# Weights loaded ahead of batch 1, and chunk 0's feed-forward ahead of and among batch 1's attention

## The chip, the cores and the metric

One core of one Trainium2 chip runs the kernel. The metric is the device time of one execution in microseconds (us); the median of three runs stands for a kernel. TensorE is called PE below, its weight load PEld, VectorE DVE, ScalarE ACT, GpSimd POOL and SyncE SP.

## The reference

Eight batches of eight heads, 576 tokens, head size 64. Attention looks back over a window of 128 tokens and has a bias that falls with distance; its output, 4608 tokens by 512, goes through a feed-forward layer with 2048 inner columns.

```python
scores = scale * np.matmul(q, k.transpose(0, 1, 3, 2))
mask = (rel >= 0) & (rel < window)
scores = np.where(mask, scores + bias[None], -1000000000.0)
attn = exp(scores - max) / sum
x = (attn @ v), heads side by side            # 4608 x 512
h = x @ w_in                                  # 512 -> 2048
g = h * np.clip(h + 3.0, 0.0, 6.0) / 6.0
out = g @ w_out                               # 2048 -> 512
```

## The kernel before, in words

**Attention** goes by head pairs g = 0 to 31, four to a batch. A window of 128 means that each block of 128 queries sees two blocks of keys, its own ("diag") and the one before ("off"). For each pair: q and k are brought to bf16 and transposed to have the head's 64 columns on the partitions (`qTb`, `kTb`); `scores` (L344) multiplies them on PE into PSUM tiles of pool `ps_sc`; ACT takes exponentials into `pd`, `po` and a small `p4buf` (L384, L409); POOL zeroes what the mask forbids (L405, L414); `values` (L444) or, in batches 0 and 1, `attend` (L456) multiplies with v on PE and divides on DVE; `back` (L471) transposes the result into `xT`, the feed-forward's input, on PE for the first batches and by a DMA transpose from SP later.

**The feed-forward** goes by chunks of 512 tokens, nine in all (`nt`). `moe_up` (L512) is one block of 128 inner columns: four matmuls into one PSUM bank, an ACT operation (L520) that reads the bank, and a DVE operation (L521) that reads both and writes `gbuf`. There are 16 ups to a chunk. Their banks are two tiles of pool `ps_h` (tag "h"), which `transposes`, `double` and late `back`s use too; chunk 0 alone also takes one of `ps_av` and `ps_o` for some (`UP_BANKS`, L510). `moe_down` (L538) is a quarter of the 16 matmuls of 128 tokens' output: 16 steps to a chunk, with `gbuf` as weights; after each fourth, DVE copies the bank to `osb` and SP stores it.

**The order of the work** is written out by hand. Every engine executes its instructions in the order in which the code issues them. `units` (L566) lists ups and downs in one line, by order strings (`ORDER`, L563: U an up of chunk nt, D a down of chunk nt − 1), and `fill(n)` (L573) issues the next n of them; an up is held back until the attention of its tokens is done. `first_batch` (L608), `second_batch` (L667) and `segment` (L717, pairs 8 to 32) place the fills among the attention's pieces. In `segment` a pair has seven places for them, `f[0]` to `f[6]`: after the scores, after each of the two diagonal exponentials, after each of the two others, and two at the end; the pieces of `values` of the pair before stand ahead of `f[2]` and `f[4]`. `FILLS` (L715) gives seven units to pairs 9 to 11 and 13 to 15, the default eight to the others.

**The loads.** Batch 0's q and k come as runs of nine tokens a partition (`load_run`, L90), v by tokens (`load_tokens`, L108). Batch 1's q and k come as float32 runs of two pairs (`load_double`, L96) on SP's queue, are cast by POOL (`prepare_double`, L224) and transposed nine blocks of 128 at a time (`wide_double`, L249). The weights come as four column groups of w_in (`load_w_in`, L165) and four row groups of w_out (`load_w_out`, L170), cast to bf16 on their way by DMAs that POOL issues: w_in 0 during batch 0's attention, w_in 1 to 3 among batch 1's preparations, w_out ahead of the last pair of batch 1. Batch 0 keeps its `pd` and `po` in the room of `w_out_sb`, batch 1 in `gbuf[1]` (`rooms`, L275).

Of the kernel before, what the change touches and what calls it, by code (L numbers as in the profile page):

```python
# [10 lines left out]
FP32 = mybir.dt.float32  # L11
# [7 lines left out]
def kernel(  # L19
# [145 lines left out]
    def load_w_in(g):  # L165
        nc.gpsimd.dma_start(
            out=w_in_sb[:, :, ts(g, 512)],
            in_=moe_w_in[:, ts(g, 512)].rearrange("(k p) f -> p k f", p=128))

    def load_w_out(g):  # L170
        nc.gpsimd.dma_start(
            out=w_out_sb[:, ts(g, 4), :],
            in_=moe_w_out[ds(g * 512, 512), :].rearrange("(m p) d -> p m d", p=128))

    def second_w_in():
        nc.gpsimd.memset(w_out_sb[:, 4, 0:1], 0.0)
        load_w_in(1)
        load_w_in(2)
# [45 lines left out]
    def prepare_double(b, dp, copies, nms="kq", early=None):  # L224
        for nm, copy in zip(nms, copies):
            pr = prs.tile([128, RT, 2 * D], BF16, tag=f"pr{nm}", name="pr2")
            for e in range(2):
                copy(out=pr[:, :, ts(e, D)],  # L228
                     in_=ldbuf["qk".index(nm)][:, ds((2 * dp + e) * RT * D, RT * D)].rearrange(
                         "p (t d) -> p t d", t=RT))  # L230
# [307 lines left out]
    def moe_down(nt, step):  # L538
        sub, part = divmod(step, 4)
        if nt == n_nt - 1 and sub == 3:  # L540
            if part == 3:
                last_rows(nt, sub)
            return
        if part == 0:
            if nt == n_nt - 1 and sub in (1, 2) or nt == 1 and sub == 0:
                ops[nt, sub] = ps_h.tile([128, d_model], FP32, tag="h", name="ops")
            else:
                ops[nt, sub] = ps_o.tile([128, d_model], FP32, tag="o", name="ops")
        for i in range(4):
            ms = part * 4 + i  # L550
            nc.tensor.matmul(ops[nt, sub], lhsT=gts[nt][:, ms, ts(sub, 128)],  # L551
                             rhs=w_out_sb[:, ms, :], start=(ms == 0), stop=(ms == n_ms - 1))
# [13 lines left out]
    units = [(0, moe_up, step) for step in range(16)]  # L566
    for nt in range(1, n_nt + 1):
        ups, downs = iter(range(16)), iter(range(16))
        for c in "".join(ORDER[0 if nt == 1 else 2 if nt == n_nt else 1]):
            units.append((nt, moe_up, next(ups)) if c == "U" else (nt, moe_down, next(downs)))  # L570
    at = [0]

    def fill(n):  # L573
        for _ in range(n):
            if at[0] == len(units):
                return
            nt, fn, step = units[at[0]]
            if fn is moe_up and done[0] < NP * (min((nt * NT + NT - 1) // S, B - 1) + 1):
                return
            fn(nt if fn is moe_up else nt - 1, step)  # L580
            at[0] += 1

    V, P, A = nc.vector.tensor_copy, nc.gpsimd.tensor_copy, nc.scalar.copy
# [24 lines left out]
    def first_batch():  # L608
        prepare(0, (V, A))
        warm_up(20)  # L610
        tables_diag(0)
        warm_up(9)
        transposes(0, (V, A))
        tables_off(0)
        scores_diag(0)
        prepare(1, (P, V))
        transposes(1, (V, V))
        scores_off(0)
        exp_full(0)
# [21 lines left out]
        for dp in range(2):  # L641
            for nm in "kq":
                load_double(1, dp, nm, nc.sync)
        load_tokens(1, "v")
# [17 lines left out]
        done[0] = NP  # L662
        fill(1)
        wide_double(1, 0, "k", A)
        fill(2)

    def second_batch():  # L667
        for g in range(NP, 2 * NP - 1):
            if g < NP + 2:
                wide_double(1, 1, "kq"[g - NP], V)  # L670
            scores_diag(g)
            exp_diag(g, 0)
            exp_diag(g, 1)
            fill(1 if g == NP + 2 else 2)
            scores_off(g)
            exp_off_full(g)
            fill(2 if g == NP + 2 else 1)
            if g == NP + 1:
                cast_tokens(1, "v")
        for i in range(4):  # L680
            load_w_out(i)
        g = 2 * NP - 1
        scores(g)
        exp_diag(g, 0)
        exp_diag(g, 1)
# [7 lines left out]
        exp_off_full(g)  # L693
        fill(1)
        attend(NP)
        fill(1)
        attend(NP + 1)
        fill(1)
        back(NP)
        attend(NP + 2)  # L700
        fill(1)
# [62 lines left out]
    with tc.manual_schedule(engines=every):  # L764
        load_run(0, "k", nc.scalar)
        load_run(0, "q", nc.sync)
        load_run(1, "k", nc.scalar)
        load_run(1, "q", nc.sync)
        for g in (2, 3):
            load_run(g, "k", nc.scalar)  # L770
            load_run(g, "q", nc.sync)
        load_tokens(0, "v")
        constants()
        memsets()
        memsets_later()
        first_batch()
        second_batch()
        fill(2)
# [33 lines left out]
```

## Time and profile before

| what | value |
|---|---|
| median of three runs | 321.34 us (320.37 to 321.56) |
| the profiled execution's own time | 320.53 us |
| its span in the trace | 318.8 us |
| PE busy | 309.7 us, 97% |
| ACT busy | 195.8 us, 61% |
| DVE busy | 173.2 us, 54% |
| POOL busy | 140.8 us, 44% |
| mean granted clock of PE | 1.0 |

The page of a profile names groups of instructions by the line of the code, the engine, the operation, and what is written from what (`hps<-xT,w_in_sb`). Rows in order of time have the start, the length of the merged group in us, the line and, in square brackets, how long the engine stood idle before it and what released it. Rows of waits have the waiting engine, line and tile, what it waited for, then the total, the number of waits and the longest in us. Matmuls are pipelined: a group's length includes the end of its last matmul, so the distance from one start to the next is the measure of what a group costs.

### The profile page before, as it was taken

To read this page: it belongs to the slowest core of one execution; us is meant where nothing else is said; L and a number is where in the kernel's file an instruction comes from. 1 tells how busy PE (TensorE), PEld (TensorE's weight loads), DVE (VectorE), ACT (ScalarE), POOL (GpSimd) and SP (SyncE) were. 2 spreads that over 40 slices of the span, in tenths; PEclk is the share of its full clock that TensorE was granted. 3 is DMA by queue.
4 is the path that set the end of the run, shared out by engine and by line. 5 is a ranking of instruction groups with operands and counts; after the bars stand their busy time and mean duration, and the time that the engine had idled before them with its cause. 6 is when DMAs were issued, how large, how long until landed. Compare 5 with 4: busy or idle time off the path is not lost.

```text
span 318.8 us, 7860 instructions
## 1 busy us (share of the span) xinstructions
PE 309.7 (97%) x3143; PEld 165.3 (52%) x3143; DVE 173.2 (54%) x338; ACT 195.8 (61%) x334; POOL 140.8 (44%) x249
## 2 busy tenths in 40 slices
PE   7879999999999999999999999999999999999996
PEld 6565465455555444444677644444444444444443
DVE  6667675554456654655565556555656455455510
ACT  3758977877767775766676667666764244244401
POOL 7465493684494776276736663663331000000000
PEclk9999999999999999999999999999999999999999
DMA  7999999999999989999999999933112100000112
GB/s 269 208 334 217 246 272 188 246 240 175 197 263 183 206 198 220 187 192 239 218 208 205 234 197 196 244 78 72 41 36 88 53 34 35 33 33 35 66 56 76
DMA packets 131428, 51.95 MB, mean 163 GB/s; under 512 B 118976, under 2 KB 123328, under 8 KB 131392
## 3 DMA queue, kind: packets, MB, share of 16 engines
q1 hardware_dynamic: 126160, 45.36, 70.2%
q0 software_dynamic: 4224, 4.19, 8.3%
q10 hardware_dynamic: 1008, 1.90, 1.7%
q8 instruction: 24, 0.39, 0.6%
q14 instruction: 12, 0.10, 0.1%
HBM read 36.70 MB, written 9.44 MB: 145 GB/s over the span
## 4 chain that ended last, share of the span: by engine, by line
PE 86%; ACT 5%; DMA 3%; DVE 2%; issue 1%; SPq 1%; POOL 0%; POOLq 0%; ACTq 0%
PE ops L551 37%; PE hps L501 36%; PE sce L364 2%; DMA ldbuf<-in_q_dram 2%; PE av L441 2%; ACT r L520 2%; PE av L433 2%; PE ops L532 1%; DVE gbuf L521 1%; PE w L153 1%; DMA xT<-avs 1%; PE tp L220 1%; PE tp L255 1%; ACT kTb L245 1%; SPq L98 1%
## 5 line engine op out<-in xcount | busy, mean ns | idle before, releaser
L521 DVE SCALAR_TENSOR_TENSOR gbuf<-r,hps 128x512 bf16<-128x512 f32 x144 | 98.8, 687 | 100.8 <-ACT r L520 99.6
L520 ACT ACTIVATE r<-hps,bias 128x512 f32<-128x512 f32 x144 | 99.0, 689 | 86.4 <-PE hps L501 86.1
L501 PE MATMUL hps<-xT,w_in_sb 128*128 128x512 bf16 (+1 forms) x640 | 145.1, 358 | 1.1 <-ACT xT L488 0.3
L551 PE MATMUL ops<-w_out_sb,gbuf 128*128 128x512 bf16 x560 | 137.8, 379 | 0.0
L501 PEld LDWEIGHTS <-w_in_sb 128*128 128x128 bf16 x640 | 59.3, 98 | 55.4 <-issue 1.3
L551 PEld LDWEIGHTS <-gbuf 128*128 128x128 bf16 x560 | 51.8, 98 | 55.5
L414 POOL TENSOR_SCALAR_AFFINE_SELECT po<-po 128x512 bf16<-128x512 bf16 x48 | 30.3, 636 | 32.9 <-ACT po L412 32.7
L405 POOL TENSOR_SCALAR_AFFINE_SELECT pd<-pd 128x512 bf16<-128x512 bf16 x48 | 29.8, 634 | 29.6 <-ACT pd L388 29.5
L388 ACT ACTIVATE pd<-sce,bias_d 128x512 bf16<-128x512 f32 x48 | 31.7, 685 | 5.3 <-POOL tbuf L195 4.0
L195 POOL CAST tbuf<-ldbuf 128x512 bf16<-128x512 f32 (+1 forms) x45 | 25.6, 614 | 19.7 <-issue 10.4
L560 DVE COPY osb<-ops 128x512 f32<-128x512 f32 x33 | 22.7, 688 | 19.7 <-PE ops L551 19.6
L412 ACT ACTIVATE po<-sce,bias_o 128x512 bf16<-128x512 f32 x48 | 33.0, 688 | 0.0
L452 DVE TENSOR_TENSOR avs<-av,rc 128x384 bf16<-128x384 f32 (+1 forms) x48 | 23.6, 491 | 1.6
L441 PEld LDWEIGHTS <-pd 128*128 128x128 bf16 x192 | 14.4, 97 | 8.3 <-issue 0.5
L433 PE MATMUL av<-vbuf,po 128*128 128x65 bf16 x192 | 18.1, 193 | 0.0
L441 PE MATMUL av<-vbuf,pd 128*128 128x65 bf16 x192 | 17.5, 194 | 0.3 <-ACT kTb L245 0.3
L433 PEld LDWEIGHTS <-po 128*128 128x128 bf16 x192 | 14.3, 98 | 3.0 <-DVE avs L452 0.5
L188 POOL CAST vbuf<-ldbuf 128x1024 bf16<-128x1024 f32 x14 | 14.2, 1043 | 3.5 <-DMA ldbuf<-in_v_dram 3.5
L417 ACT ACTIVATE p4buf<-sce,bias_d 128x64 bf16<-128x64 f32 x48 | 15.5, 323 | 0.0
L228 POOL CAST pr<-ldbuf 128x576 bf16<-128x576 f32 x20 | 12.9, 670 | 5.0 <-DMA ldbuf<-in_q_dram 2.1
L451 DVE RECIPROCAL rc<-av 128x6 f32<-128x6 f32 (+1 forms) x48 | 8.8, 183 | 4.3 <-PE av L441 4.3
L364 PEld LDWEIGHTS <-kTb 64*32 64x32 bf16 x736 | 6.2, 91 | 8.7 <-issue 7.6
(104 smaller groups left out, 211.7 us busy)
## 6 DMA issues: line engine op xcount, KB each, us to landing
out_dram<-osb SPq DMA_DIRECT2D x33, 256.0 KB, 2.5
ldbuf<-in_v_dram SPq DMA_DIRECT2D x32, 256.0 KB, 5.2
ldbuf<-in_q_dram SPq DMA_DIRECT2D x20, 256.0 KB, 4.7
ldbuf<-in_k_dram SPq DMA_DIRECT2D x16, 256.0 KB, 4.8
ldbuf<-in_q_dram SPq DMA_DIRECT2D x12, 288.0 KB, 7.2
ldbuf<-in_k_dram SPq DMA_DIRECT2D x12, 288.0 KB, 6.5
w_in_sb<-in_moe_w_in_dram POOLq DMA_DIRECT2D x4, 512.0 KB, 9.3
w_out_sb<-in_moe_w_out_dram POOLq DMA_DIRECT2D x4, 512.0 KB, 10.4
```

The costliest lines, as they stand in the source:

```text
L195: nc.gpsimd.tensor_copy(out=tbuf[:m, :, j, :], in_=s[:m, j, :, :].rearrange("p (i e) d -> p i (e d)", e=2))
L388: nc.scalar.activation(out=pd[:, e, :, :], in_=st["sce"][e][:, :, 0, :], func=ACT.Exp, bias=bias_d[:, h:h + 1], scale=scale)
L405: nc.gpsimd.affine_select(out=pd[:, e, :, :], in_=pd[:, e, :, :], pattern=[[0, 4], [1, 128]], channel_multiplier=-1, base=0, compare_op=AL ...
L412: nc.scalar.activation(out=po[:, e, :, :], in_=sc[:, :, 1, :], func=ACT.Exp, bias=bias_o[:, h:h + 1], scale=scale)
L414: nc.gpsimd.affine_select(out=po[:, e, :, :], in_=po[:, e, :, :], pattern=[[0, 4], [-1, 128]], channel_multiplier=1, base=-1, compare_op=A ...
L433: nc.tensor.matmul(out_av, lhsT=po[:, e, qt % 4 if full(g) else qt - 1, :], rhs=vb[:, qt - 1, h, :], start=True, stop=False)
L441: nc.tensor.matmul(out_av, lhsT=d, rhs=vb[:, qt, h, :], start=(qt == 0), stop=True)
L452: nc.vector.tensor_tensor(out=st[g, "avs"][:, qts[0]:qts[0] + nq, :, :], in0=av[:, 0:nq, :, 0:D], in1=rc[:, 0:nq, :, :].to_broadcast([128, ...
L501: nc.tensor.matmul(hps[:, lo:hi], lhsT=w_in_sb[:, ks, ts(ms, 128)], rhs=xT[:, ks, ds(src, hi - lo)], start=(ks == 0), stop=(ks == n_ks - 1))
L520: nc.scalar.activation(out=r6, in_=hps, func=ACT.Relu, bias=bias3[:, 0:1], scale=1.0 / 6.0)
L521: nc.vector.scalar_tensor_tensor(out=gts[nt][:, ms, :], in0=r6, scalar=1.0, in1=hps, op0=ALU.min, op1=ALU.mult)
L551: nc.tensor.matmul(ops[nt, sub], lhsT=gts[nt][:, ms, ts(sub, 128)], rhs=w_out_sb[:, ms, :], start=(ms == 0), stop=(ms == n_ms - 1))
```

## The change

All four groups of w_in are now issued by POOL during batch 0's attention, and all four of w_out right behind batch 0's last `back`. Batch 1's q and k follow on the same queue, pair by pair, as runs that the DMA casts to bf16 (`cast_run`), and are transposed in blocks of 64 by `transposes`, which batch 0 already uses. Batch 1's v and batch 2's q and k are loaded by SP after a one-element POOL copy that reads pair 5's k.

Chunk 0's 16 ups are issued in one `fill(16)` ahead of batch 1, its downs in `FIRST`'s order ahead of and among batch 1's attention; the fills between batch 1's attends go. Banks of some downs change (`BESIDE`, and `ps_av` for odd 128s of chunk 0). In the new order strings U is an up of the chunk, d a down of the same chunk, D one of the chunk before. Pairs 8 to 12 get six units, 13 to 24 seven, 25 on eight.

```diff
+    crun = ctx.enter_context(tc.tile_pool(name="crun", bufs=4))
...
+    def cast_run(g, nm):
+        b, hp = divmod(g, NP)
+        pr = crun.tile([128, RT * D], BF16, tag=f"cr{nm}", name="cr")
+        nc.gpsimd.dma_start(out=pr, in_=src_of[nm][b, 2 * hp:2 * hp + 2, :, :].rearrange(
+            "e (p t) d -> (e p) (t d)", t=RT))
+        st[g, nm] = pr
...
-    ORDER = [("UUDUDUUDUD", "UUDUDUDUD", "UDUDUDD", "UUDDDD"),
-             ("DDDD", "UUDUDUDUD", "UUDUDUDUD", "UUDUDUDDUU"),
-             ("DDDD",) * 4]
...
+    BESIDE = {(1, 1), (1, 3), (2, 1), (3, 0), (4, 0), (n_nt - 1, 1), (n_nt - 1, 2)}
+    FIRST = [0, 4, 1, 5, 2, 6, 3, 7, *range(8, 16)]
...
+    units = [(0, moe_up, step) for step in range(16)] + [(0, moe_down, step) for step in FIRST]
+    late = "DDDD", "UUDUDUDUDUUDUDUDUDUUDUDUDDUU"
+    early = {1: "UUUUd" * 4 + "d" * 12, 2: "UUUUd" * 4 + "d" * 8, 3: "UUUUD" * 4 + "d" * 8,
+             4: "UUD" * 8 + "dddd", 5: late[1], n_nt: "D" * 16}
...
+        for i in range(1, 4):
+            load_w_in(i)
...
-        prepare_double(1, 0, (P, P), early=second_w_in)
...
-        wide_double(1, 0, "q", V)
-        prepare_double(1, 1, (P, P))
-        load_w_in(3)
+        for i in range(4):
+            load_w_out(i)
+        for g in range(NP, 2 * NP):
+            for nm in "kq":
+                cast_run(g, nm)
+        nc.gpsimd.tensor_copy(out=ldbuf[3][0:1, 0:1], in_=st[NP + 1, "k"][0:1, 0:1])
+        load_tokens(1, "v")
...
+        fill(16)
...
+        fill(8)
+        transposes(NP, (V, A))
...
+            if g < 2 * NP - 1:
+                transposes(g + 1, (V, V))
...
-    FILLS = {g: (1, 1, 1, 2, 0, 1, 1) for g in (9, 10, 11, 13, 14, 15)}
+    FILLS = {g: (1, 1, 1, 1, 0, 1, 1) for g in range(8, 13)}
+    FILLS |= {g: (1, 1, 1, 2, 0, 1, 1) for g in range(13, 25)}
```

More of the change, by code (lines that the diff above doesn't have):

```diff
@@ L173, in load_w_out @@
             in_=moe_w_out[ds(g * 512, 512), :].rearrange("(m p) d -> p m d", p=128))
[L175 to L178, printed above, removed]
     def cast_v(b, j, copy):
@@ L544, in moe_down @@
         if part == 0:
-            if nt == n_nt - 1 and sub in (1, 2) or nt == 1 and sub == 0:
+            if (nt, sub) in BESIDE:
                 ops[nt, sub] = ps_h.tile([128, d_model], FP32, tag="h", name="ops")
+            elif nt == 0 and sub % 2 == 1:
+                ops[nt, sub] = ps_av.tile([128, d_model], FP32, tag="av", name="ops")
             else:
@@ L561, in moe_down @@
                 nc.sync.dma_start(out=out[rows, :], in_=osb)
-    ORDER = [("UUDUDUUDUD", "UUDUDUDUD", "UDUDUDD", "UUDDDD"),
-             ("DDDD", "UUDUDUDUD", "UUDUDUDUD", "UUDUDUDDUU"),
-             ("DDDD",) * 4]
-    units = [(0, moe_up, step) for step in range(16)]
+    BESIDE = {(1, 1), (1, 3), (2, 1), (3, 0), (4, 0), (n_nt - 1, 1), (n_nt - 1, 2)}
+    FIRST = [0, 4, 1, 5, 2, 6, 3, 7, *range(8, 16)]
+    steps = [iter(range(16)) for _ in range(n_nt)], [iter(range(16)) for _ in range(n_nt)]
+    units = [(0, moe_up, step) for step in range(16)] + [(0, moe_down, step) for step in FIRST]
+    late = "DDDD", "UUDUDUDUDUUDUDUDUDUUDUDUDDUU"
+    early = {1: "UUUUd" * 4 + "d" * 12, 2: "UUUUd" * 4 + "d" * 8, 3: "UUUUD" * 4 + "d" * 8,
+             4: "UUD" * 8 + "dddd", 5: late[1], n_nt: "D" * 16}
     for nt in range(1, n_nt + 1):
-        ups, downs = iter(range(16)), iter(range(16))
-        for c in "".join(ORDER[0 if nt == 1 else 2 if nt == n_nt else 1]):
-            units.append((nt, moe_up, next(ups)) if c == "U" else (nt, moe_down, next(downs)))
+        for c in early.get(nt, late[0] + late[1]):
+            at = nt - (c == "D")
+            units.append((at, moe_up, next(steps[0][at])) if c == "U" else
+                         (at, moe_down, next(steps[1][at])))
     at = [0]
@@ L579, in fill @@
                 return
-            fn(nt if fn is moe_up else nt - 1, step)
+            fn(nt, step)
             at[0] += 1
@@ L640, in first_batch @@
         cast_v(0, 4, P)
[L641 to L644, printed above, removed]
+        for i in range(1, 4):
+            load_w_in(i)
         attend(0)
@@ L662, in first_batch, with second_batch @@
         done[0] = NP
+        fill(16)
+    def second_batch():
+        fill(8)
+        transposes(NP, (V, A))
         fill(1)
[L664 to L670, printed above, removed]
+        for g in range(NP, 2 * NP):
             scores_diag(g)
@@ L673, in second_batch @@
             exp_diag(g, 1)
-            fill(1 if g == NP + 2 else 2)
+            if g < 2 * NP - 1:
+                transposes(g + 1, (V, V))
+            fill(1)
             scores_off(g)
             exp_off_full(g)
[L677 to L685, printed above, removed]
+            fill(2 if g == NP else 1 if g < 2 * NP - 1 else 0)
+            for j, copy in {NP: (), NP + 1: ((0, V), (1, P)), NP + 2: ((2, V),),
+                            NP + 3: ((3, V), (4, P))}[g]:
+                cast_v(1, j, copy)
         prepare_double(2, 0, (P, P))
@@ L777 @@
         second_batch()
-        fill(2)
         segment(2 * NP, G, lambda g: FILLS.get(g, (1, 1, 1, 2, 0, 1, 2)))
```

5 lines of the change are left out of this document (removed).

## Prediction

> **What bounds the kernel now.** I read the page first (busy shares, slices), then PE's own waits, then PE, ACT and DVE side by side in the order of time, last the queue of SP.
>
> ```profile
> span 318.8 us, 7860 instructions
> PE 309.7 (97%) x3143; PEld 165.3 (52%) x3143; DVE 173.2 (54%) x338; ACT 195.8 (61%) x334; POOL 140.8 (44%) x249
> PE   7879999999999999999999999999999999999996
> ...
> PE scd L297 <- DVE kTb L221: 0.9, 3, 0.4
> ...
> PE av L441 <- ACT kTb L245: 0.3, 2, 0.2
> ...
> PE hps L501 <- DVE gbuf L521: 0.3, 1, 0.3
> ...
> PE hps L501 <- DMA xT<-avs: 0.3, 1, 0.3
> ...
> PE tp L255 <- POOL pr L228: 0.2, 1, 0.2
> PE tb L482 <- DVE avs L452: 0.2, 1, 0.2
> PE tp L243 <- ACT kTb L245: 0.2, 1, 0.2
> ```
>
> The reader is to see that PE is the bound: 97% busy, and of its waits the largest group has 0.9 us in three, the longest 0.4 (the rows left out are smaller, but for 1.4 us at the very start). The work of PE stays nearly the same under the change, so the change can win very little, and every wait that it makes on PE is lost for good: nothing after it makes up for it. So the question is only which waits go and which come.
>
> The unit of the feed-forward part is one up (four matmuls of L501) or one down (four of L551).
>
> ```profile
> 301.83 10.36 PE ops L551 x48
> ```
>
> 48 downs' matmuls in 10.36 us are 0.216 us each, 0.863 us for a unit. An up also needs ACT and DVE before its PSUM bank is free again:
>
> ```profile
> 52.81 1.03 PE L501 MATMUL hps<-xT,w_in_sb 128*128 128x512 bf16 x4
> 53.68 0.44 PE L243 MATMUL tp<-ident,pr 128*128 128x128 bf16 x5
> ...
> 55.34 1.89 PE L501 MATMUL hps<-xT,w_in_sb 128*128 128x512 bf16 x8
> ...
> 53.88 0.69 ACT L520 ACTIVATE r<-hps,bias 128x512 f32<-128x512 f32 x1 [1.33 <-PE hps L501]
> ...
> 54.60 0.69 DVE L521 SCALAR_TENSOR_TENSOR gbuf<-r,hps 128x512 bf16<-128x512 f32 x1 [1.24 <-ACT r L520]
> ```
>
> This is the row that decides my forecast. The up that starts at 52.81 gives PE away at 53.68. ACT takes it 0.20 later (53.88), for 0.69; DVE 0.03 after that (54.60), for 0.69, to 55.29; and the next up in that bank starts at 55.34. So **a bank is back 1.66 us after its up's last matmul**. Pool "h" has two banks. Two ups in a row are free; a third needs the first one's bank, and only one up (0.863 us) lies between: it waits 0.80 us unless other PE work lies there. The old order strings never have three ups in a row, and a down always belongs to the chunk before.
>
> **The change part by part.**
>
> *The order of the units from g 8 on.* This is the large term. The strings for chunks 1 and 2 are now "UUUUd" four times and then 12 or 8 downs: four ups in a row in two banks, and then a down of the same chunk, whose fourth matmul has as weights what DVE writes for the up just before it. That down waits 1.66 − 3 × 0.216 = 1.0 us if nothing lies between. What lies between is the attention of a head pair, and it also puts its exponentials into ACT's queue:
>
> ```profile
> 128.82 0.46 PE L364 MATMUL sce<-qTb,kTb 64*32 64x160 bf16 x32
> ...
> 130.97 0.23 PE L441 MATMUL av<-vbuf,pd 128*128 128x65 bf16 x2
> ...
> 136.78 0.46 PE L364 MATMUL sce<-qTb,kTb 64*32 64x160 bf16 x32
> ...
> 131.75 0.68 ACT L388 ACTIVATE pd<-sce,bias_d 128x512 bf16<-128x512 f32 x1
> 132.32 0.69 ACT L412 ACTIVATE po<-sce,bias_o 128x512 bf16<-128x512 f32 x1
> 132.89 0.33 ACT L417 ACTIVATE p4buf<-sce,bias_d 128x64 bf16<-128x64 f32 x1
> 133.19 0.69 ACT L520 ACTIVATE r<-hps,bias 128x512 f32<-128x512 f32 x1
> ```
>
> A head pair takes 136.78 − 128.82 = 7.96 us with eight units, so its attention costs PE 7.96 − 8 × 0.863 = 1.06 us: 0.41 of scores, the rest in two pieces of about 0.33 (values). On ACT a large operation follows the last one after 0.57 to 0.58 us, the small one takes 0.30.
>
> I walk g 13 (order U U U U d U U), from the end of its scores. Up 0 runs 0 to 0.86, its bank is free at 2.47 + 0.05. Up 1 ends at 1.73, values at 2.08. Up 2 needs bank 0 and starts at 2.52: **0.44 lost**; ends 3.38. On ACT the first exponential pushes up 1's activation to 2.22, so DVE is done with it at 3.62; up 3 starts at 3.65: **0.27 lost**; ends 4.51. Its activation stands behind up 2's and behind an exponential with its small one, starts at 5.05, and DVE ends at 6.46; the down's first three matmuls end at 5.16, the fourth starts at 6.51: **1.35 lost**. Ups 4 and 5 find free banks. Sum 2.06 us. By the same steps g 14 (U U d U U U U) loses 0.40 + 1.00 + 0.55 = 1.95 and g 15 (d U U U U d d) 0.60 + 0.45 + 0.35 + 0.70 = 2.1. In g 8 to 10 six units stand in a pair and half a double transpose takes an "h" bank too: g 8 (U U d U U U) 1.4 + 1.0 + 0.8 = 3.2; g 9 (U d U U U U) 0.1 + 0.65 + 0.45 + 0.65 = 1.85; g 10 (d U U U U d) 0.3 + 0.85 + 1.5 = 2.65. Chunk 3's "UUUUD" takes its downs from the chunk before, so only the banks count: g 17 to 19 lose 0.73, 1.14, 0.80. "UUD" (g 21 to 24) loses 0.1 a pair as an estimate, 0.5; the pairs with downs alone nothing. Sum 7.7 + 6.1 + 2.7 + 0.5 = **17.0 us**. Its bounds: 0, if what lies between always covers the 0.80 and the 1.0; and 24, if nothing does (seven and a half blocks of four ups with their own down at 1.8, four of chunk 3 at 0.8, 17 in all) and the exponentials ahead of the activations add 0.6 us to each block (7). I take the walk, which lies between them.
>
> *Waits that go with the old order:* the last quoted 0.3 (xT), 0.3, 0.2 and 0.2 are in or at that stretch, **−1.0**.
>
> *The front, to the first scores of batch 2.* The casts on POOL go, and with them the waits of 0.2 (pr) and 0.3 (gbuf L521): −0.5. The four wide transposes become 36 narrow ones a head pair:
>
> ```profile
> 13.45 0.76 PE L220 MATMUL tp<-ident,pr 64*64 64x64 bf16 x36
> 14.14 0.20 PE L323 MATMUL sco<-qTb,kTb 64*128 64x64 bf16 x2
> ...
> 24.62 0.67 PE L255 MATMUL tp<-ident,pr 128*128 128x128 bf16 x9
> 25.13 1.24 PE L501 MATMUL hps<-xT,w_in_sb 128*128 128x512 bf16 x5
> ...
> 48.30 0.21 DVE L462 RECIPROCAL rcw<-wide 128x10 f32<-128x10 f32 x1
> 48.55 0.82 DVE L463 TENSOR_TENSOR avs<-wide,rcw 128x640 bf16<-128x640 f32 x1
> ```
>
> 4 × 0.69 against 4 × 0.51: +0.8 (with the first one's start). Sixteen ups in a row have four banks, and fit but for the last, whose bank was used two ups before: +0.8. The four attends of batch 1 lose the ups between them; DVE needs 0.21 + 0.82 for each and PE some 0.8, and the first two now wait for the last exponentials of g 7: +1.3. Sum **+2.4**.
>
> *The transfers.* w_in and w_out leave ahead of batch 1. All descriptors go through POOL's queue; SP's loads of batch 1 v and batch 2 wait behind a POOL copy that waits for g 5's k.
>
> ```profile
> L166 POOL DMA_DIRECT2D w_in_sb<-in_moe_w_in_dram x4: 742/746/887, 12.5 to 28.3; - x4
> ...
> DMA to landing us min/median/max: 8.9/9.3/12.4
> ...
> L171 POOL DMA_DIRECT2D w_out_sb<-in_moe_w_out_dram x4: 750/764/770, 41.3 to 43.6; - x4
> ...
> DMA to landing us min/median/max: 6.7/10.4/14.2
> ```
>
> Four w_out issued together landed between 41.3 + 6.7 = 48.0 and 43.6 + 14.2 = 57.8, 3.3 us apart. w_in 0 lands by 12.5 + 8.9 = 21.4 or sooner; seven more at 3.3 put w_out 3 at 44.5. PE asks for it about 42 (ups from 23 for 14 us, six downs). So 0 to 2.6; the loads of batch 1 that ran beside the old w_in are gone, so I take 0. If that cover is gone the chunk's downs wait, up to 2.6.
>
> **Sum:** 17.0 − 1.0 + 2.4 = 18.4 us on the profiled execution's 320.53 (span 318.80 and 1.73 around it): **339**. The median of the runs, 321.34, is 0.8 higher, which I do not add; a measurement tells 0.5%, about 1.6 us, from no change.
>
> **The rivals.**
>
> *SP's queue holds PE instead.* For it: that queue has hardly a gap.
>
> ```profile
> 120.79 1.61 SPq L475 DMA_TRANSPOSE xT<-avs  x1
> 122.45 4.49 SPq L112 DMA_DIRECT2D ldbuf<-in_k_dram  x5
> 127.06 4.80 SPq L200 DMA_TRANSPOSE qTb<-tbuf  x1
> ...
> 152.22 1.61 SPq L475 DMA_TRANSPOSE xT<-avs  x1
> ```
>
> A batch takes it 31.4 us. With seven units a pair PE without bank waits would need 4 × (1.06 + 6.04) = 28.4, and would wait about 2.7 for xT at the starts of chunks 4 and 5: 2.4 + 5.4 − 1.0, **327** (324 to 331). Against it: the banks alone already make chunk 2's batch 34.5 and chunk 3's 31.1.
>
> *Not slower: the attention pieces cover the banks.* One mechanism: at L517's pool "h", if what lies between an up and the next but one is 0.80 us beyond the up itself, no bank wait is left. For it: ACT's pace of 0.58 and DVE's 0.69 are under PE's 0.863. Against: the pieces are 0.33 and 0.41. With the front's additions covered as well by its four banks and downs, −0.5 − 1.0: **319**.
>
> *The change doesn't get its order: the weights are late.* If the seven loads after w_in 0 came 4.7 us apart and not 3.3, w_out 3 would land at 54.3 and the downs would wait 12 us from 42: **351**. Against it: the 3.3 was measured while SP loaded v beside it.
>
> *PE loses its pace.* At the start it ran at half of it, 0.11 a matmul against 0.056 later, though the page's clock says 1.00.
>
> ```profile
> 1.43 2.32 PE L153 MATMUL w<-ident 128*128 128x128 bf16 x20 [1.43 <-POOL ident masks.py:199]
> ...
> 18.84 0.45 PE L482 MATMUL tb<-ident,avs 128*128 128x128 bf16 x5 [0.27 <-DVE avs L463]
> ...
> 10.00:20.00 10.00, 8.40 (x198) 5.80 (x194) 6.75 (x13) 6.67 (x7) 4.55 (x8) 1.00 1.13 224
> ```
>
> If idle pieces of 1 us brought that back for a quarter of the 41 us of matmuls in g 8 to 15, it would cost 10 us more: **349**. Against: with 1.6 of 10 us idle the pace held at 18.84; g 13 would idle 2.1 of 9.1. The Trainium skill, "TensorE: Matmul & The Clock Gate", section "A second HAM failure mode: psum-queue depth-cycling", says that PE which idles briefly between groups as it goes round PSUM banks can swing between half and full clock; this trace shows no such swing, and no row of it has bank waits this dense.
>
> **How the numbers follow.** Forecast (own range 331 to 346) 0.62; SP's queue 0.17; not slower 0.11; late loads 0.05; lost pace 0.05. The range runs from 323 (the lower end of the SP case) to 346; outside lie the not-slower case and most of the last two. Of the 0.11, 0.06 falls under 319.7 and 0.05 within 0.5%; slower 0.89.
>
> **What would show it.** Right: PE waits on DVE gbuf at the ups and on the weights of the downs of several us in all; PE's slices at 7 and 8 in g 8 to 10 and 13 to 15, about 68 to 95 and 109 to 137 us; the pairs with downs alone at full pace. Wrong: those slices at 9; PE waiting for the xT transposes at chunk starts with SP without a gap (the SP case); a PE gap of several us near 40 us (late loads); matmuls of 512 columns 0.43 us apart (lost pace).

## The result, and the profile after

The changed kernel takes **343.27 us** (median of four runs, 342.48 to 345.63) beside 321.45 for the kernel before: ratio 1.069, 95% interval 1.062 to 1.076. Its profiled execution took 343.46 us. Forecast were 339.0, range 323 to 346. Of its four executions three, at a mean granted clock of 0.999 or 1.0, took 342.48 to 343.46; the fourth, at 0.995, took 345.63.

The page of the changed kernel: span, PE's busy time, PE's busy tenths and granted clock in 40 slices of 8.5 us. Lines of the code have moved by 3 to 5: an up is now L504, its ACT operation L523, its DVE operation L524, a down L556.

```profile
span 341.7 us, 8065 instructions
...
PE 315.2 (92%) x3251; PEld 166.0 (49%) x3251; DVE 177.1 (52%) x345; ACT 195.1 (57%) x334; POOL 139.2 (41%) x248
...
PE   8889999777889888999999998999999999999996
...
PEclk9999999999999999999999999999999999999999
```

PE is still the engine with most to do, but it is 92% busy, not 97%, in a span 22.9 us longer. Its slices at 7 and 8, past the start, lie at 60 to 102 and 111 to 137 us, with one more at 205 to 214; forecast were 68 to 95 and 109 to 137. The first stretch begins sooner because batch 1's attends lie in it, and the single slice holds two waits for xT (below). PE's waits in the changed kernel (total, times, longest):

```profile
PE hps L504 <- DVE gbuf L524: 8.2, 18, 1.3
PE ops L556 <- DVE gbuf L524: 5.1, 7, 1.0
PE hps L504 <- DMA xT<-avs: 2.4, 4, 0.8
...
PE sce L367 <- DMA kTb<-tbuf: 0.7, 1, 0.7
```

The first two rows had 0.3 together before. Stage by stage (the window, its length, then PE's busy time and the other engines'), in the changed kernel:

```profile
68.88:96.91 28.03, 21.74 (x218) 10.51 (x217) 14.55 (x26) 21.12 (x38) 15.95 (x27) 1.00 0.75 150
96.91:110.42 13.51, 13.51 (x171) 7.24 (x170) 4.61 (x11) 7.55 (x15) 7.54 (x12) 1.00 0.88 218
110.42:138.35 27.93, 23.55 (x253) 10.87 (x253) 15.85 (x30) 19.28 (x35) 14.73 (x28) 1.00 1.00 187
138.35:145.46 7.11, 7.11 (x84) 3.58 (x83) 2.05 (x5) 2.83 (x6) 7.11 (x13) 1.00 0.31 100
145.46:170.00 24.54, 22.33 (x250) 10.90 (x249) 15.00 (x29) 18.50 (x34) 11.05 (x20) 1.00 1.14 190
...
177.10:207.43 30.33, 28.97 (x394) 20.56 (x393) 17.52 (x35) 21.26 (x40) 18.27 (x33) 1.00 1.17 199
```

These are pairs 8 to 10, 11 and 12, 13 to 15, 16, 17 to 19, and 21 to 24. PE idles 6.3, 0, 4.4, 0, 2.2 and 1.4 us in them: most in the pairs that hold four ups in a row, less where two ups and a down take turns (21 to 24), and not at all in those that hold only downs. In the three stretches with four ups in a row the busiest of the other engines is ScalarE, at 75%, 69% and 75%. One of those stalls, pair 13, PE, ACT and DVE in order of time:

```profile
113.89 2.18 PE L504 MATMUL hps<-xT,w_in_sb 128*128 128x512 bf16 x8 [0.33 <-DVE gbuf L524]
115.91 0.90 PE L556 MATMUL ops<-w_out_sb,gbuf 128*128 128x512 bf16 x3
117.78 0.39 PE L556 MATMUL ops<-w_out_sb,gbuf 128*128 128x512 bf16 x1 [0.97 <-DVE gbuf L524]
...
116.31 0.69 ACT L523 ACTIVATE r<-hps,bias 128x512 f32<-128x512 f32 x1
...
117.03 0.69 DVE L524 SCALAR_TENSOR_TENSOR gbuf<-r,hps 128x512 bf16<-128x512 f32 x1 [0.68 <-ACT r L523]
```

The third up waits 0.33 for its bank. The down's first three matmuls are through by 116.8; the fourth needs as weights what DVE ends at 117.72, and starts at 117.78. The eight matmuls in the first row last 2.18 us, where 8 × 0.216 and the last one's end are 1.89: the fourth up lost 0.29 too.

**The balance.** The first scores of batch 2 (pair 8) divide the span. First the row of the kernel before, then, in order of time, rows of the changed kernel's front.

```profile
51.40 0.58 PE L336 MATMUL sce<-qTb,kTb 64*128 64x256 bf16 x8
```

```profile
36.86 1.02 PE L504 MATMUL hps<-xT,w_in_sb 128*128 128x512 bf16 x4 [0.64 <-DVE gbuf L524]
37.72 7.07 PE L556 MATMUL ops<-w_out_sb,gbuf 128*128 128x512 bf16 x32
...
60.16 0.22 PE L444 MATMUL wide<-vbuf,gbuf 128*128 128x65 bf16 x2 [0.48 <-ACT gbuf L401]
...
61.56 0.19 PE L444 MATMUL wide<-vbuf,gbuf 128*128 128x65 bf16 x1 [0.78 <-POOL vbuf L178]
...
62.98 0.45 PE L485 MATMUL tb<-ident,avs 128*128 128x128 bf16 x5 [0.63 <-DVE avs L466]
...
68.88 0.58 PE L339 MATMUL sce<-qTb,kTb 64*128 64x256 bf16 x8
```

Pair 8 starts 17.48 us later, after 16 downs more, which are worth 16 × 0.863 = 13.81: the front costs 3.7. From there to the end the kernel before took 318.8 − 51.4 = 267.4, less the same 13.8 that is 253.6; the changed one 341.7 − 68.9 = 272.8. So **19.2 of the 22.9 us are lost from pair 8 on**.

### The profile page after: what moved, and what is told of

It reads as the page before. It is cut to its first block, busy times and chain, and to the rows that moved or that the text cites. A ratio compares the mean times of both kernels' runs of the same rounds, so it can differ in the third digit from the quotient of the medians.

```text
span 341.7 us, 8065 instructions
## 1 busy us (share of the span) xinstructions
PE 315.2 (92%) x3251; PEld 166.0 (49%) x3251; DVE 177.1 (52%) x345; ACT 195.1 (57%) x334; POOL 139.2 (41%) x248
## 4 chain that ended last, share of the span: by engine, by line
PE 71%; ACT 10%; DVE 8%; DMA 6%; issue 3%; POOL 1%; SPq 0%; DVEq 0%; POOLq 0%
PE ops L556 30%; PE hps L504 29%; ACT r L523 5%; DVE gbuf L524 5%; DMA xT<-avs 4%; DMA kTb<-tbuf 2%; PE sce L367 2%; PE tp L216 1%; PE av L444 1%; ACT po L415 1%; PE av L436 1%; ACT pd L391 1%; PE tb L485 1%; PE ops L535 1%; DVE avs L455 1%
## 5 line engine op out<-in xcount | busy, mean ns | idle before, releaser
L504 PE MATMUL hps<-xT,w_in_sb 128*128 128x512 bf16 (+1 forms) x640 | 142.6, 357 | 11.6 <-DVE gbuf L524 8.2
L523 ACT ACTIVATE r<-hps,bias 128x512 f32<-128x512 f32 x144 | 99.0, 689 | 94.6 <-PE hps L504 94.0
L524 DVE SCALAR_TENSOR_TENSOR gbuf<-r,hps 128x512 bf16<-128x512 f32 x144 | 98.8, 687 | 97.1 <-ACT r L523 96.6
L556 PE MATMUL ops<-w_out_sb,gbuf 128*128 128x512 bf16 x560 | 137.6, 379 | 5.2 <-DVE gbuf L524 5.1
L504 PEld LDWEIGHTS <-w_in_sb 128*128 128x128 bf16 x640 | 60.1, 97 | 69.1 <-issue 17.4
L556 PEld LDWEIGHTS <-gbuf 128*128 128x128 bf16 x560 | 51.7, 98 | 64.2 <-DVE gbuf L524 9.7
L184 POOL CAST vbuf<-ldbuf 128x1024 bf16<-128x1024 f32 x12 | 12.2, 1043 | 0.0
L491 ACT COPY xT<-tb 128x576 bf16<-128x576 bf16 x8 | 5.1, 640 | 11.0 <-PE tb L485 11.0
L367 PE MATMUL sce<-qTb,kTb 64*32 64x160 bf16 (+1 forms) x736 | 10.5, 229 | 0.7 <-DMA kTb<-tbuf 0.7
```

What stands on the lines that cost most here:

```text
L504: nc.tensor.matmul(hps[:, lo:hi], lhsT=w_in_sb[:, ks, ts(ms, 128)], rhs=xT[:, ks, ds(src, hi - lo)], start=(ks == 0), stop=(ks == n_ks - 1))
L523: nc.scalar.activation(out=r6, in_=hps, func=ACT.Relu, bias=bias3[:, 0:1], scale=1.0 / 6.0)
L524: nc.vector.scalar_tensor_tensor(out=gts[nt][:, ms, :], in0=r6, scalar=1.0, in1=hps, op0=ALU.min, op1=ALU.mult)
```

## The experiments

Twelve kernels, each timed beside the kernel before on its chip. The ratio is to that kernel. The kernel before had medians of 320.75 to 322.47 beside them, so the differences in us in the text, between medians taken at different times or on different chips, are good to 1 or 2 us. By the ratios run 8's 9.4 would be 11.1, run 11's 1.8 would be 2.9 and run 5's 15.0 would be 14.8. A small gain counts only where the trace shows the wait that went.

| kernel | us (median of four) | ratio, 95% interval |
|---|---|---|
| the changed kernel | 343.27 | 1.069 (1.062 to 1.076) |
| 1 VectorE off the bank | 339.54 | 1.055 (1.049 to 1.061) |
| 2 early downs read the other gbuf | 337.76 | 1.050 (1.042 to 1.059) |
| 3 first ups read older xT | 340.43 | 1.057 (1.052 to 1.063) |
| 4 the three together | 334.04 | 1.038 (1.032 to 1.044) |
| 5 a lag of 8 downs | 328.28 | 1.023 (1.018 to 1.029) |
| 6 VectorE beside ScalarE | 346.27 | 1.080 (1.071 to 1.089) |
| 7 the same, older xT | 341.93 | 1.065 (1.059 to 1.070) |
| 8 ScalarE off the chain | 333.83 | 1.034 (1.030 to 1.039) |
| 9 the loads in the old order | 330.01 | 1.024 (1.020 to 1.028) |
| 10 lag of 8, two downs carried | 329.51 | 1.023 (1.018 to 1.027) |
| 11 downs between the attends | 341.45 | 1.060 (1.051 to 1.068) |
| 12 lag of 8 to the end | 326.39 | 1.012 (1.006 to 1.018) |

The theory: PE waits for PSUM banks and for weights just made, because the order puts ups in fours and a down right behind the up that feeds it. Rivals: SP's queue, the loads, PE's pace.

### 1. VectorE off the bank

```diff
-        nc.vector.scalar_tensor_tensor(out=gts[nt][:, ms, :], in0=r6, scalar=1.0, in1=hps,
+        nc.vector.scalar_tensor_tensor(out=gts[nt][:, ms, :], in0=r6, scalar=1.0, in1=r6,
```

> VectorE's step behind an up multiplies ScalarE's result by itself and reads no PSUM bank (the multiplication by the up's own value is left out), so that a bank of the pool is back after ScalarE's 0.69 us and not after ScalarE's 0.69 and VectorE's 0.69. Theory 'banks': the third and fourth up of a run wait no more; PE's wait of 8.2 us at ups for VectorE's gbuf goes nearly to nothing, the downs' wait of 5.1 for gbuf stays or grows by 1 to 2 (PE is there sooner). 335.0 to 337.5 us beside the changed kernel's 343.3. Rival 'SP': the transposes that SP issues bound the stretch, the waits come back at xT and kTb: 340 or more. Rival 'pace': PE itself is slower in short pieces, its waits are a result: 341 or more.

Measured 339.5: 3.7 less, not 6 to 8. The ups' wait did go (0.7 us is left, now for ScalarE), but others came. PE's waits and the groups of DVE and POOL (busy time, mean ns of one) in this kernel:

```profile
PE ops L556 <- DVE gbuf L524: 7.5, 13, 1.2
...
PE av L436 <- POOL po L417: 2.4, 3, 0.8
```

```profile
L524 DVE SCALAR_TENSOR_TENSOR gbuf<-r 128x512 bf16<-128x512 f32 x144 | 109.6, 768 | 82.5 <-ACT r L523 81.6
...
L408 POOL TENSOR_SCALAR_AFFINE_SELECT pd<-pd 128x512 bf16<-128x512 bf16 x48 | 33.4, 710 | 39.6 <-ACT pd L391 39.5
```

and the same two groups in the changed kernel:

```profile
L524 DVE SCALAR_TENSOR_TENSOR gbuf<-r,hps 128x512 bf16<-128x512 f32 x144 | 98.8, 687 | 97.1 <-ACT r L523 96.6
...
L408 POOL TENSOR_SCALAR_AFFINE_SELECT pd<-pd 128x512 bf16<-128x512 bf16 x48 | 30.0, 635 | 49.5 <-ACT pd L391 48.5
```

Both engines became slower: VectorE's step 768 ns instead of 687, GpSimd's unchanged selects 710 instead of 635. VectorE now reads two operands from SBUF and none from PSUM. The Trainium skill, "SBUF — State Buffer", section "🔬 SBUF: two separate sides", says that such a VectorE operation and a GpSimd one that reads SBUF exclude each other at a shared port pair; the two means agree. So this edit took the wait away and brought a new one: its 3.7 is no clean price of the banks.

### 2. Early downs read the other gbuf

```diff
+        gt = gbuf[(nt + 1) % 2] if nt in (1, 2) and sub == 0 else gts[nt]
...
-            nc.tensor.matmul(ops[nt, sub], lhsT=gts[nt][:, ms, ts(sub, 128)],
+            nc.tensor.matmul(ops[nt, sub], lhsT=gt[:, ms, ts(sub, 128)],
```

> The first four downs of chunks 1 and 2, each of which stands right behind the up that makes its fourth weight, take their weights from the other chunk's gbuf, which is long there (so these outputs are of other data). Theory 'banks and fourth weights': the downs' wait of 5.1 us goes and little of it comes back at the ups, since a bank needs 1.66 us and a down and an up last 1.73: 338.0 to 340.0 us. Rival 'SP': 342 or more, the waits for xT grow. Rival 'the ups take it back': the run of four ups behind it waits longer for its banks by what the down no longer waits, ups' wait 11 or more instead of 8.2, time 342 or more.

Measured 337.8, 5.5 less, a little more than the 3.3 to 5.3 expected. The downs' wait is gone, and the ups' stayed (8.6 after 8.2): the rival that the ups take it back falls.

### 3. First ups read older xT

```diff
-        at0 = nt * NT % RING
+        at0 = (nt - (nt > 1 and ms < 2)) * NT % RING
```

> The first two ups of each chunk from 2 on read the chunk before's columns of xT (other data), so that they don't wait for the transposes of the batch that has just ended. Theory 'latency': 0.8 to 1.7 us at each of three or four chunk starts are only the way from VectorE's avs over SP's transpose to xT with nothing ahead of it on PE; 1.7 us of ups cover it: 340.0 to 341.5 us, the wait of 2.4 for xT goes to under 0.8. Rival 'SP's queue': the transposes are late because SP is full; the third up then waits as long, time 342.5 or more.

Measured 340.4, 2.8 less, as the waits for xT said (2.4, and 0.16 more for each of four, below). Nothing of it came back: the ups' and downs' waits are 8.2 and 5.1 as before.

### 4. The three together

> The three edits together (nothing multiplied by the up's own value, the eight early downs and the first two ups of a chunk read other data). Theory 'banks, fourth weights and latency': the sum of the three, 343.3 less 7, 4.5 and 2.5: 327.5 to 331.0 us; what stays above the kernel before (321.4) is the front, 3.7, and some idle at scores. Rival 'SP': once PE is fast again, SP's transposes hold it: 331 to 337, with xT and kTb waits above 6 us. Rival 'pace': above 337.

Measured 334.0, 9.2 less, where the three alone sum to 12.1; by number inside the rival SP's 331 to 337, but with no wait for xT or kTb above 0.2 us, where that rival asked for more than 6. What came instead is GpSimd's masks, and behind them the clock: windows of this kernel (length, PE busy, the others, then PE's granted clock) and a row of PE:

```profile
149.40:152.10 2.70, 0.75 (x6) 0.30 (x4) 1.66 (x2) 1.27 (x2) 2.70 (x4) 1.00 1.88 189
152.10:155.30 3.20, 3.19 (x13) 1.35 (x14) 0.98 (x3) 0.95 (x2) 1.38 (x3) 0.51 0.89 200
```

```profile
152.42 3.88 PE L504 MATMUL hps<-xT,w_in_sb 128*128 128x512 bf16 x10
```

GpSimd is busy all of the first window, with selects at 734 ns; PE works 0.75 of 2.70 us. Then the clock is at 0.51, and ten matmuls of ups take 3.88 us instead of 2.3. A second such place follows at 182 to 190 us, and all four executions had a mean clock of 0.99. At half speed 3.2 us lose 1.6; two of them are about what the sum lacks. The Trainium skill, "TensorE: Matmul & The Clock Gate", section "What's actually happening", has PE at half clock after an idle window of some 3.4 us; here 2.7 us at 28% busy were enough.

### 5. A lag of 8 downs

```diff
-    FIRST = [0, 4, 1, 5, 2, 6, 3, 7, *range(8, 16)]
+    FIRST = [0, 4, 1, 5, 2, 6, 3, 7]
...
-    early = {1: "UUUUd" * 4 + "d" * 12, 2: "UUUUd" * 4 + "d" * 8, 3: "UUUUD" * 4 + "d" * 8,
+    early = {**{n: "UUD" * 8 + "d" * 8 for n in (1, 2, 3)},
...
-    FILLS |= {g: (1, 1, 1, 2, 0, 1, 1) for g in range(13, 25)}
+    FILLS |= {g: (1, 1, 1, 2, 0, 1, 1) for g in range(21, 25)}
```

The rest follows from it: banks, and four downs instead of eight ahead of batch 1's transposes. All of the reference is computed.

> The loads and chunk 0's ups stay ahead, but only 8 of chunk 0's downs run ahead, and from there each chunk's ups go two by two with a down of the chunk before (a lag of 8 downs), with eight units in the pairs 13 to 20; all of the computation is done. Theory 'banks and fourth weights': the walk's 17.0 goes; the front's 3.7 stays, the waits for xT at the starts of chunks (2.4 to 3) too, and batch 1's attention, with 8 downs fewer beside it, may lose 0 to 3: 325 to 331 us; ups' and downs' waits for gbuf under 1.5 together. Rival 'SP': 331 or more, as PE at its old pace meets late transposes. Rival 'the loads': what is lost is lost to the loads and the front, so that the order gives nothing back: 337 or more.

Measured 328.3, **15.0 less**, with the loads and chunk 0's ups where the change put them. Of the 13.3 us of waits for gbuf 1.1 are left, at 25.44 and 36.59 us, ahead of pair 8; from pair 8 on none of the 12.2 is listed any more:

```profile
PE hps L504 <- DMA xT<-avs: 1.6, 2, 0.8
...
PE hps L504 <- DVE gbuf L524: 1.1, 2, 0.6
```

```profile
62.12 0.58 PE L339 MATMUL sce<-qTb,kTb 64*128 64x256 bf16 x8
```

Eight downs more than the kernel before (6.9 us) stand ahead of pair 8, so the front costs 62.12 − 51.40 − 6.90 = 3.8, as in the changed kernel; from pair 8 on 3.9 are lost instead of 19.2. This is the run that settles the large term: the order of the units was worth 15 us, by real work and not by work left out. With it go eight units a pair in pairs 13 to 20 and other banks for some downs; that the listed waits for gbuf went from 12.2 to none is what ties the gain to the order. The rival that the loads cost the time falls, and the front keeps its 3.8.

### 6 and 7. VectorE beside ScalarE

```diff
-        nc.vector.scalar_tensor_tensor(out=gts[nt][:, ms, :], in0=r6, scalar=1.0, in1=hps,
-                                       op0=ALU.min, op1=ALU.mult)
+        nc.vector.tensor_scalar(out=gts[nt][:, ms, :], in0=hps, scalar1=1.0, scalar2=0.0,
+                                op0=ALU.min, op1=ALU.max)
```

> VectorE takes the minimum of the up itself, out of its bank, beside ScalarE and not behind it (the product of the two is left out): a bank is back, and the weight is there, about 0.94 us after the up's last matmul and not 1.66, and VectorE reads one operand, from PSUM. Theory 'banks and fourth weights': the ups' 8.2 us go, of the downs' 5.1 some 3.6: 331 to 335 us. The first experiment brought 3.7 and not 6 to 8, because the downs' wait grew by 2.4 and because GpSimd's selects took 710 ns and not 635 while VectorE read two operands from SBUF, which put 2.4 of waits for the masks behind it: if that is so, the selects take about 635 ns here and PE's waits for them stay under 1.0. Rival 'pace of the attention': PE, once free of its waits, is too fast for ScalarE and GpSimd at seven units a pair, the waits for the masks are 2 or more here too, at 635 ns a select: 334 to 338.

Measured 346.3: a miss, no gain at all. The group of VectorE says why:

```profile
L524 DVE TENSOR_SCALAR gbuf<-hps 128x512 bf16<-128x512 f32 x144 | 99.2, 691 | 98.9 <-ACT r L523 98.4
```

It still started when ScalarE ended, though it reads nothing that ScalarE writes: the two read the same bank. The Trainium skill, "PSUM — Partial Sum Buffer", section "PSUM bank collisions raise a hardware error ⚠️", says that two engines may not be at one bank at once, reads included, and that the compiler's scheduler puts them one behind the other; the 98.4 us agree. So the chain of 1.66 us stayed, with the waits (8.9 and 5.3), and the run tells only that other arithmetic on VectorE brings nothing. Run 7 added the edit of run 3:

> As the one before, and the first two ups of a chunk read the chunk before's columns of xT. Theory 'banks, fourth weights, latency': 2 to 3 less than that one: 328 to 332 us. Rival 'pace of the attention': the kernel with all three edits kept 334.0 because GpSimd's masks came late at the seven-unit pairs, not because its selects were slowed: 332 to 335, with waits for masks of 3 to 5 us around 149, 183 and 217 us.

Measured 341.9, by the medians 4.3 less than run 6 where 2 to 3 were expected; as run 6 didn't cut the chain, it tells nothing of run 4's shortfall. The selects were at 632 ns in both, so it is the second SBUF operand, and not the edit as such, that slowed GpSimd in runs 1 and 4. Two of run 6's four executions had a mean clock of 0.99 and 0.995; its two at 1.0 took 344.07 and 344.96. Beside those, run 7, at 1.0 throughout, is 2.6 less, as expected, and run 6 is some 1.5 us slower than the changed kernel, not 3. That 1.5 stays unexplained; the intervals overlap.

### 8. ScalarE off the chain

```diff
-        nc.scalar.activation(out=r6, in_=hps, func=ACT.Relu, bias=bias3[:, 0:1], scale=1.0 / 6.0)
+        nc.scalar.activation(out=r6.rearrange("p (h s c) -> p h s c", h=2, s=2), in_=tab[:, 0:2, :, :],
+                             func=ACT.Relu, bias=bias3[:, 0:1], scale=1.0 / 6.0)
```

> ScalarE's step behind an up reads a table in SBUF and not the up's bank (the relu of the up is left out, the product with the up stays), so that only VectorE's 0.69 us hold the bank, with VectorE's operands where they are in the changed kernel, one in SBUF and one in PSUM. In the kernel 'side by side' VectorE still started at ScalarE's end (98.4 us of its idle time), so the chain was not cut there; here it is. Theory 'banks and fourth weights': of the ups' 8.2 us and the downs' 5.1, 11 to 12 go: 330.5 to 334.0 us, GpSimd's selects at about 635 ns. Rival 'pace of the attention': the waits for masks come up, 2 us or more, at selects of 635 ns: 334 to 338. Rival 'pace of PE': 340 or more.

Measured 333.8, **9.4 less**, in the range of the theory. PE's waits in this kernel:

```profile
PE hps L504 <- DMA xT<-avs: 4.3, 5, 1.6
PE ops L557 <- DVE gbuf L525: 2.5, 4, 1.0
...
PE hps L504 <- DVE gbuf L525: 1.7, 2, 1.1
```

With one step of the chain gone, ups and downs wait 4.2 us instead of 13.3, and GpSimd's selects kept their 634 ns: this is the cleaner price. The waits for xT grew by 1.9, and here SP's queue is behind more than half of them:

```profile
165.57 2.26 SPq L478 DMA_TRANSPOSE xT<-avs  x1
...
190.53 4.42 SPq L113 DMA_DIRECT2D ldbuf<-in_q_dram  x5
195.06 2.36 SPq L478 DMA_TRANSPOSE xT<-avs  x1
```

From 136 to 199 us SP has no gap above 0.12 us. The transpose at 195.06 stands behind the loads, 4.85 us after VectorE had ended its avs (190.21); so does one at 162.97 (avs at 158.03), and one at 198.16 starts 1.2 late. PE's waits of 0.60, 1.02 and 0.80 for xT, 2.4 of the 4.3 us, come right behind these three. That is the predicted rival's mechanism. The longest wait, 1.55 at 170.09, is not of this kind: the transpose ahead of it, at 165.57, starts 0.12 after its avs and lasts 2.26 where most last 1.23; why is open.

### 9. The loads in the old order

The order strings, banks and `FILLS` of the kernel before, with the change's loads of w_in and of batch 1; w_out goes behind batch 1's scores, six ups ahead of batch 1's attention, the other ten among it.

> The new loads of w_in and of batch 1 (k and q cast by the DMA) with the units in the order of the kernel before: chunk 0's ups beside batch 1's attention, six of them ahead of it, the downs a chunk behind, w_out loaded behind batch 1's scores. Theory 'order': the loads cost what the units that cover them lack later, 1 to 4 us at batch 1's attention, and nothing from batch 2 on: 322 to 326 us. Rival 'loads': what the changed kernel lost it lost to its loads: 330 or more.

Measured 330.0: outside the theory's range, and at the rival's bound. Split at pair 8, little of it is shown to be lost to the loads, though. PE's waits and the row of pair 8:

```profile
PE tp L216 <- DVE gbuf L524: 1.5, 2, 0.8
...
PE hps L504 <- DVE qTb L217: 1.3, 2, 1.2
PE tp L216 <- DMA cr<-in_q_dram: 1.0, 1, 1.0
```

```profile
57.78 0.58 PE L339 MATMUL sce<-qTb,kTb 64*128 64x256 bf16 x8
```

The front costs 57.78 − 51.40 = 6.4 with the same units ahead of it, and the rest 327.2 − 57.8 − 267.4 = 2.0. Of the front's waits only 1.0 is for a load. Most are between ups and the transposes of batch 1, which go through the same two "h" banks and through VectorE and ScalarE: a loss of the order that I wrote for this run. So from pair 8 on the loads cost 2.0 at most, with 0.2 of PE's waits there for w_out; what they would cost in a well-made front it leaves open.

### 10 and 12. What is left with a lag of 8

Run 10 takes run 5 and gives pairs 8 and 12 a unit less (`FILLS[8] = FILLS[12] = (1, 1, 1, 0, 0, 1, 1)`), so that two downs stand ahead of each later chunk's first up.

> The kernel with a lag of 8 and two downs fewer before the starts of the chunks (one unit fewer in pairs 8 and 12), so that two downs of the chunk before stand ahead of each chunk's first up. Theory 'latency': 1.7 us of downs cover the way of xT at the starts, the wait of 1.6 for xT and the idle before ups at 192 to 195 us (2.0) go: 326.0 to 327.5 us beside 328.3. Rival 'SP's queue': the transposes come later by what PE no longer waits: 328 or more.

Measured 329.5, no gain: a miss. The wait for xT fell from 1.6 to 0.6, and that of the scores for kTb rose from 0.5 to 1.5. Run 12 keeps the lag and eight units a pair to the end:

```diff
-    early = {**{n: "UUD" * 8 + "d" * 8 for n in (1, 2, 3)},
-             4: "UUD" * 8 + "dddd", 5: late[1], n_nt: "D" * 16}
+    early = {**{n: "UUD" * 8 + "d" * 8 for n in range(1, n_nt)}, n_nt: "D" * 8}
...
-    FILLS |= {g: (1, 1, 1, 2, 0, 1, 1) for g in range(21, 25)}
```

> The kernel with a lag of 8 (328.3), with this lag and eight units a pair kept from pair 13 to the end, so that no pair has seven. Theory 'seven-unit pairs': in that kernel the waits of 3.5 us between 178 and 196 us (xT 2.0, kTb 0.65, po 0.4, and a few) came where pairs have seven units, 6.9 us a pair, so that the attention's chain over ScalarE, GpSimd and SP's transposes, which before had 7.7, set the end; at eight units they go: 324.5 to 326.5 us. Rival 'latency at the starts of chunks': each chunk's first ups still stand right behind the last transposes of a batch, the waits stay, or move to the later chunks: 327.5 or more.

Measured 326.4, 1.9 less than run 5 (by the ratios 3.7), at the upper end of what was expected. Pairs 21 to 24 in run 5, and then in run 12 (length, PE busy):

```profile
169.29:201.81 32.52, 29.86 (x372) 19.05 (x377) 17.70 (x36) 21.32 (x40) 19.32 (x35) 1.00 1.18 197
```

```profile
170.60:203.47 32.87, 32.30 (x385) 19.77 (x384) 18.35 (x37) 21.45 (x40) 18.98 (x33) 1.00 1.10 204
```

Four units more fit into almost the same time: PE's idle 2.7 us went to 0.6. So in both runs the four pairs take some 32.5 us whether PE has 28 units to do or 32, and with 28 it waits. It stays over the kernel before (ratio 1.012), and no run came below it.

### 11. Downs between the attends

```diff
-        fill(8)
+        fill(4)
         transposes(NP, (V, A))
...
+        fill(1)
         attend(NP)
+        fill(1)
         attend(NP + 1)
+        fill(1)
         back(NP)
         attend(NP + 2)
+        fill(1)
         back(NP + 1)
```

> The changed kernel with four of chunk 0's downs taken from ahead of batch 1's attention and put between the values of batch 1 (one ahead of each attend, one ahead of the second transposition back). Theory 'front': the 3.1 us that PE waits between 58 and 66 us are the chain of values, VectorE's division and the transposition with nothing beside them; three of the four places that get a down lose their wait, and the DMA's casts have landed before they are read: 340.5 to 342.0 us. Rival 'casts': with four downs fewer ahead, PE comes before the casts of k and q, a wait of 1 or more for cr, time 343 or more. Rival 'the ups take it back': what is won at the front is lost at the first ups of chunk 1, since they wait for xT, 342.5 or more.

Measured 341.5, 1.8 less, in the expected range, though the intervals of the two ratios overlap. The trace is plainer:

```profile
66.36 0.58 PE L339 MATMUL sce<-qTb,kTb 64*128 64x256 bf16 x8
```

Pair 8 starts 2.5 us sooner with the same units done, and the waits quoted above at 60.16, 61.56 and 62.98 are gone. From pair 8 on the two kernels take the same (272.4 and 272.8), so nothing was given back; no wait for a cast came up.

## Why the prediction was right, point by point

- **The order of the units, 17.0: right in place, and nearly in size.** The view of waits has 8.2 + 5.1, of which 1.1 (two waits) belong to the front, so 12.2. It counts an up or down as busy to its last matmul's end (1.02 us, against 0.863 from start to start), so each of the 23 waits is 0.16 longer in truth: 12.2 + 3.7 = 15.9. Pair 13, forecast to lose 0.44, 0.27 and 1.35, lost 0.49, 0.29 and 1.13 by the rows above. By stages the walk gave 7.7, 6.1, 2.7 and 0.5; PE's idle in the windows, counted short in the same way, is 6.3, 4.4, 2.2 and 1.4. Run 5 took 15.0 back with the order alone, runs 2 and 8 show the two parts (5.5 for the downs' weights; 9.4 for both with one link of the chain cut).
- **Old waits gone, −1.0: about right.** From pair 8 on the kernel before lists three waits, 0.3 + 0.3 + 0.2 = 0.8, and the changed kernel none of them; the fourth, 0.2 of `tp` for kTb, lies ahead of pair 8 and is still there.
- **The front, 2.4: too small; it was 3.7.** The last of 16 ups lost 0.64 + 0.16 = 0.80, as worked out; an early one, at 25.70, lost 0.42, though the step had all but the last fit. What failed is "The four attends of batch 1 lose the ups between them … +1.3": run 11 got 2.5 back there. The step left out that the second attend waits 0.78 for GpSimd's cast of the last piece of batch 1's v:

```profile
60.90 0.60 POOL L178 CAST vbuf<-ldbuf 64x512 bf16<-64x512 f32 x1
```

  It stands behind the masks of batch 1's last pair (59.60 to 60.95), for which GpSimd had waited 2.49 for ScalarE's exponentials. The load of v is not the cause: GpSimd cast another piece of it at 53.33.
- **w_out lands in time, 0: right.** 32 matmuls of downs run 7.07 us from 37.72 without a gap (32 × 0.216 and the last one's end).
- **Missing from the sum: waits for xT and kTb at the starts of chunks**, 2.4 + 0.7 and 0.16 for each of five, 3.9 in all. The old order has four downs ahead of a chunk's first up, the new strings begin with the up. Run 3 took 2.8 of it away. The three together, 15.9 − 0.8 + 3.9 = 19.0, are the 19.2 lost from pair 8 on but for 0.2; with the front, 22.9. So 339.0 came out 4.3 low on the runs' median. It was some luck that it was not more: 3.9 left out and 1.3 too little for the front stand against 1.1 too much in the walk.
- **SP's queue as the rival (327): not the main bound, but there.** Two of the five waits for xT and kTb have SP idle for 1.6 us ahead of the transpose for which PE then waited: 0.31 at 147.00 (rows below) and 0.68 at 179.13. SP's queue and PE of the changed kernel:

```profile
142.59 0.36 SPq L566 DMA_DIRECT2D out_dram<-osb  x1
144.51 1.20 SPq L478 DMA_TRANSPOSE xT<-avs  x1
...
147.00 1.24 PE L504 MATMUL hps<-xT,w_in_sb 128*128 128x512 bf16 x5 [0.31 <-DMA xT<-avs]
...
200.28 4.23 SPq L113 DMA_DIRECT2D ldbuf<-in_q_dram  x5
204.62 1.25 SPq L478 DMA_TRANSPOSE xT<-avs  x1
```

  The other three, 0.67 for kTb at 200.30 and 0.63 and 0.78 for xT at 209.08 and 210.23, have SP without a gap above 0.12 us from 176 to 208; the transpose at 204.62 stands behind the loads, 5.0 us after VectorE had ended its avs (199.65). So the rival's mechanism was at work for 2.1 of the 3.1 us, about a tenth of what was lost, and run 8 met more of it as soon as the banks were quicker. I gave the two as alternatives; they go together.
- **Attention covers the banks (319), weights late (351):** neither. The pieces of attention left 15.9 us uncovered.
- **PE loses its pace (349): not in the profiled execution, and little in any.** The clock is 0.9 or more in all 40 slices and 32 matmuls run at 0.216 each, with PE idle a fifth of pairs 8 to 10. But the mechanism exists, in run 4 and in the front that this kernel shares with run 2. Run 2's granted clock by slices of 8.4 us:

```profile
PEclk9999999799999999999999999999999999999999
```

  The 7 is at 59 to 67 us, batch 1's attends: there the clock was at 0.50 for some 3 us behind PE's waits of 0.48, 0.78 and 0.63, the same three that left it at 1.00 in the changed kernel's profiled execution. The changed kernel's slowest execution, at a mean clock of 0.995, may have met the same: 0.005 of its 343.9 us are 1.7 us (an estimate; it has no trace).

Open: what the three pieces of the front's wait are each worth, and why four pairs take 32.5 us in runs 5 and 12 (SP's queue is full there, but run 10's has a gap of 1.7 us near 190 us and was no faster).

## What to carry to other kernels

When PE is at 97%, read how long a PSUM bank is away (here 1.66 us: two engines, one behind the other) and lay out the order so that PE has that much other work between an up and the second up behind it, and between an up and the first use of what it makes; a lag of a few downs was worth 15 us. Waits don't add up when they go together: three edits that were worth 12.1 us singly gave 9.2, since GpSimd's masks and the clock behind them were next in line. An experiment that takes a wait away can change a second thing (operands from SBUF, the clock), so read the mean times of the untouched engines first.

## What the runs showed of the hardware that was not expected

- VectorE with both operands in SBUF and GpSimd's selects slowed each other: 687 to 768 ns and 635 to 710 ns (run 1), 734 for the selects in run 4, and 632 to 636 in the runs in which VectorE read one operand from PSUM.
- PE's granted clock fell to 0.51 for 3.2 us behind 2.7 us in which PE was 28% busy (run 4); in pairs 8 to 15 of the changed kernel waits of up to 1.3 us with an up or down between them left it at 1.00.
- The same waits need not give the same clock: with PE idle 0.48, 0.78 and 0.63 us in batch 1's attends it stayed at 1.00 in the changed kernel's trace and fell to 0.50 for some 3 us in run 2's.
